# An MLP kernel's start: two weight pieces on ACT's DMA queue, and a shorter row of filling products

## The chip, the cores and the metric

The kernel runs on one core of one Trainium2 chip. The metric is the device time of one execution in microseconds; lower is better. The engines are TensorE (PE, with its weight loads shown as PEld), VectorE (DVE), ScalarE (ACT), GpSimd (POOL) and SyncE (SP), which issues the transfers here. Transfers are carried out by 16 DMA engines that all queues share.

## The reference

A layer norm without parameters, a product with `w1`, a bias, a GELU (tanh form), a product with `w2` and a bias. All tensors are bf16.

```python
B, S, D, F = 1, 2048, 1024, 3584

def reference(x, w1, b1, w2, b2):
    y = _layernorm(x, axis=-1)
    h = _gelu(jnp.einsum("bsd,df->bsf", y, w1) + b1)
    return jnp.einsum("bsf,fd->bsd", h, w2) + b2
```

## The kernel before

The 2048 rows are cut into 16 tiles of 128 rows, and four tiles make a block of 512. For each block the first product makes 28 rows of `hT` (each 128 features by 512 columns, the sum over 8 pieces of D), ACT applies bias and GELU, and the second product makes each tile's output in two halves of 512 columns. DVE adds the second bias and SyncE stores the result. TensorE runs first product, second product, first product and so on, block by block.

The kernel writes a program for each engine by hand: an operation is put at the end of its engine's list with the events that it waits for, and `_emit` (line 74) turns the lists into instructions in that order. Nothing reorders them afterwards, except that DVE's later work is merged by estimated times (line 626 and on).

Only the start matters for this change. It goes like this:

- **Loads.** `LOADS` (line 32) is the order in SyncE's queue behind x tiles 0 and 1. Numbers are pieces of `w1`, negative numbers are x tiles (-2 is tile 2), and `"b1"` is the first bias, which waits for a clearing by GpSimd. The helper `dma` (line 185) records every load, so all have the line L186; it takes a queue `q` and uses SyncE's if there is none. Pieces 0 to 3 hold, for the first, second, third and fourth 128 rows of D, the 1024 columns for the first eight feature rows. Pieces 4 to 7 hold the same rows of D for the next eight feature rows, and pieces 8 to 15 the other four 128-row parts of D. Each of these pieces is 256 KB, as each x tile is. Later pieces are larger.
- **ACT** begins with `preload_act_table` (line 428), which loads the table of the GELU. Behind it stand the sums of tiles 0 and 1 (line 431), each waiting for its x tile; ACT and DVE (line 434) sum a part each.
- **DVE** subtracts the mean from tiles 0 and 1, a part at a time (`centre`, line 439).
- **TensorE** first does filling products on a constant (`fill`, line 295; their result is not used). `fill(n, k)` makes n products of k x 128 columns. Before the change there are nine of 512 columns. Then it turns the first two 128-column parts of tile 0 (`pe_T`, line 300, products with an identity, L311), does two filling products of 128 columns, and follows `OPEN` (line 23). `OPEN` is the list of what TensorE does first: `("T", t, g)` turns a group of parts of tile t, and `(g, t0, t1, d0, d1)` runs the products (L339) of feature group g on tiles t0 to t1 for the parts d0 to d1 of D. So the order is: turn tile 1's first group; eight products of 128 columns with piece 0 on tile 0; turn the second groups of tiles 0 and 1; eight products of 128 columns with piece 0 on tile 1; then 24 products of 256 columns with pieces 1, 2 and 3; then 32 with pieces 4 to 7; then pieces 8 to 11.
- The last four parts of D of tiles 0 and 1 aren't turned by TensorE: DVE turns them in 32 x 32 blocks (line 448), and DVE and ACT move the blocks to their places (`move_half`, line 489, recorded as L494). DVE's twelve of these copies stand behind `mean_tile(2)` (line 478), which waits for x tile 2. The products with pieces 8 to 11 wait for the copies.
- ACT copies each turned group from PSUM to `yT_sb` (L317).

Of the kernel before, what the change touches and what calls it, by code (L numbers as in the profile page):

```python
# [11 lines left out]
P = 128  # L12
# [4 lines left out]
UGROUPS = ((0, 4), (4, 8), (8, 10), (10, 11), (11, 12))  # L17
NPAIR = 2 * UGROUPS[-1][1]
NCEN = 2
N_FILL_A = 9  # L20
N_FILL_C = 2
JT = 4
OPEN = (("T", 1, 0), (0, 0, 1, 0, 1), ("T", 0, 1), ("T", 1, 1), (0, 1, 2, 0, 1), (0, 0, 2, 1, JT), (1, 0, 2, 0, JT),
# [5 lines left out]
          ((0, 2, 6), (2, JT, 4)))  # L29
ACT_BLOCKS_01 = ((0, 1), (0, 2), (1, 2), (1, 3))  # L30
ACT_BLOCKS = ((0, 1), (0, 2), (0, 3), (1, 2), (1, 3), (2, 3))
LOADS = (0, 1, 2, "b1", 3, 4, -2, 5, 6, 7, 8, 9, 10, -3) + tuple(range(11, 22))
NOB = 2
TAIL_CUTS = (0, 384, 512)
N_W2_CHUNKS = 2
# [58 lines left out]
def bass_standalone__mixer_channel_mlp__prompt_kernel(  # L94
# [46 lines left out]
    w1v = w1.rearrange("(t p) f -> p t f", p=P)  # L141
    w2v = w2.rearrange("(t p) d -> p t d", p=P)

    with ExitStack() as es:
        sb = lambda name, shape, dt: es.enter_context(nc.sbuf_tensor(name, shape, dt))

        w1_sb = sb("w1_sb", [P, DT, F], BF16)
# [28 lines left out]
        act = _Prog("s_act")  # L176
# [8 lines left out]
        def dma(dst, src, sig, nbytes, q=None):  # L185
            (q or sp).op(lambda e, dst=dst, src=src: e.dma_start(dst, src), sig=sig, sem="d_" + sig, inc=16)  # L186
            dma_bytes[0] += nbytes
            est[sig] = DMA_T0 + dma_bytes[0] / DMA_BYTES_PER_US

        def load_x_tile(i, q=None):  # L190
            dma(x_sb[:, i, :], xf[i * P:(i + 1) * P, :], f"x{i}", P * D * 2, q)
            x_ev[i] = f"x{i}"
# [4 lines left out]
            for i in range(b0 * TPB, b1 * TPB):  # L197
                x_ev[i] = f"xb{b0}"

        def load_w1(ci):  # L200
            j0, j1, a, b = w1_chunks[ci]
            dma(w1_sb[:, j0:j1, a:b], w1v[:, j0:j1, a:b], f"w1c{ci}", (j1 - j0) * P * (b - a) * 2)

        def load_w2(ci):
            dma(w2_sb[:, ci * W2C:(ci + 1) * W2C, :], w2v[:, ci * W2C:(ci + 1) * W2C, :], f"w2c{ci}",
# [2 lines left out]
        for i in range(2):  # L208
            load_x_tile(i)
        for o in LOADS:  # L210
            if o == "b1":
                sp.op(None, waits=["b1z"])
                dma(b1r_sb[0:FT, :], b1.rearrange("(t p) -> t p", p=P), "b1", F * 2)
            elif o < 0:
                load_x_tile(-o)
            else:
                load_w1(o)
        assert n_open == 1 + max(o for o in LOADS if o != "b1")
        for ci in range(n_open, len(w1_chunks)):
            load_w1(ci)  # L220
# [74 lines left out]
        def fill(n, k):  # L295
            rhs = one.unsqueeze(1).broadcast_to([P, k, P])
            for _ in range(n):
                pe.op(lambda e: e.matmul(ps[:, 0, 0:k * P], lhsT=one, rhs=rhs, start=True, stop=True))  # L298

        def pe_T(i, group, src):  # L300
            blk, t = divmod(i, TPB)
            j0, j1, bank = group
            bap = psb[:, bank, :]
            evs = yT_ev.setdefault(i, [None] * DT)
            for j in range(j0, j1):
                waits = []
                if j == j0:
                    waits = ["ident"] + ([bank_read[bank]] if bank in bank_read else [])
                if j == j0 or y_ev[i][j] != y_ev[i][j - 1]:
                    waits.append(y_ev[i][j])  # L310
                pe.op(lambda e, j=j, o=(j - j0) * P: e.transpose(  # L311
                    out=bap[:, o:o + P], in_=src[:, j * P:(j + 1) * P], identity=ident[:, :]),
                    waits=waits, sig=(f"tp{i}_{j0}" if j == j1 - 1 else None))
                evs[j] = f"te{i}_{j0}"
            psrc = bap[:, 0:(j1 - j0) * P].rearrange("p (j s) -> p j s", j=j1 - j0)
            dst = yT_sb[:, blk % 2, j0:j1, t * P:(t + 1) * P]
            act.op(lambda e, dst=dst, psrc=psrc: e.copy(out=dst, in_=psrc), waits=[f"tp{i}_{j0}"], sig=f"te{i}_{j0}")  # L317
            bank_read[bank] = f"te{i}_{j0}"
            pe_t[0] += (j1 - j0) * 0.056
# [106 lines left out]
            store_last[(ob, region)] = sev  # L426

        act.op(lambda e: e.preload_act_table(ACT.Gelu_apprx_tanh))
        def sums(i, na):
            n2 = (D - na) // 2  # L430
            act.op(lambda e: e.activation(out=hT_sb[:, 2 * NRAW + i, 0:na], in_=x_sb[:, i, 0:na], func=ACT.Copy,
                                          scale=1.0 / D, accum_out=sum_sb[:, 2 * i:2 * i + 1]),
                   waits=[f"x{i}"], sig=f"sa{i}")
            return (lambda e: e.tensor_tensor_reduce(out=o_sb[:, i, 0:n2], in0=x_sb[:, i, na:na + n2],  # L434
                                                     in1=x_sb[:, i, na + n2:D], op0=ALU.add, op1=ALU.add,
                                                     scale=1.0 / D, scalar=0.0, accum_out=sum_sb[:, 2 * i + 1:2 * i + 2]),
                    [f"x{i}"], f"sd{i}")

        def centre(i, j0, j1):
# [4 lines left out]
            y_ev.setdefault(i, []).extend([f"y{i}_{j0}"] * (j1 - j0))  # L444

        sd = [sums(0, SA0), sums(1, HC)]
        def turn_half(i):
            dve_put((lambda e: e.transpose(out=hT_sb[:, NPAIR - 4 + i, :], in_=c_sb[:, i, JT * P:D]), y_ev[i][JT:DT],
# [74 lines left out]
        for q in range(4):  # L523
            f = q ^ 1
# [3 lines left out]
        for h in range(2):  # L528
            f = h ^ 1
# [10 lines left out]
            move(dve, 2, 2, tq, q)  # L540

        fill(N_FILL_A, TPB)
        pe_T(0, GROUPS[0][0], c_sb[:, 0, :])
        fill(N_FILL_C, 1)
        pe_t[0] = T_PE_START
# [81 lines left out]
        ci = fi = 0  # L627
# [57 lines left out]
```

## Time and profile before

| | us |
|---|---|
| median of 3 runs | 396.84 (396.80 to 396.92) |
| the profiled execution, its own time | 396.88 |
| span of that execution, first to last instruction | 395.6 |
| TensorE busy in the span | 392.7 (99%) |
| DVE, ACT busy | 155.6 (39%), 94.4 (24%) |
| granted TensorE clock | 1.00 |
| bytes moved | 23.64 MB, most of them in the first 55 us |

The span is what the profile covers. 1.28 us of the execution's time lie outside of it. The profile has, among other views, the chain of work that ended last, a timeline of each engine, the DMA issues with their time from issue to landing, and the busy time of each engine in a stretch. An instruction group there is named by its line (L339 is line 339 of the kernel), its engine, and the tiles that it writes and reads.

### The profile page before, as it was taken

What the parts mean: (1) busy time and instruction counts of PE and PEld (TensorE: products, weight loads), DVE (VectorE), ACT (ScalarE), POOL (GpSimd) and SP (SyncE); (2) the same over time, 40 slices, a digit from 0 to 9 for tenths busy, and PEclk for the clock granted to TensorE, in tenths of its full rate; (3) what the DMA queues carried; (4) which work ended last, traced back from release to release, by engine and by line L of the source; (5) the groups of instructions that cost most, each with busy time, mean ns of one, the idle gap of its engine ahead of it and who ended that gap; (6) DMA issues with size and microseconds to landing.
All of it is one profiled execution on the core that took longest, in us unless ns stands there. A gap on an engine that the chain in (4) does not pass through costs nothing.

```text
span 395.6 us, 4775 instructions
## 1 busy us (share of the span) xinstructions
PE 392.7 (99%) x2039; PEld 197.6 (50%) x2039; DVE 155.6 (39%) x344; ACT 94.4 (24%) x169; POOL 10.8 (3%) x31
## 2 busy tenths in 40 slices
PE   8999999999999999999999999999999999999998
PEld 5888844444444444444444444444444444444445
DVE  5998989989996005987100000001100000001011
ACT  6787520000144332000023443100003334400000
POOL 1202000110002000000000000000000000000000
DMA  8999940000000000000000000000000000000000
GB/s 284 377 366 384 386 148 22 17 29 13 27 2 0 0 2 0 29 23 17 28 13 0 2 0 0 15 13 27 25 16 15 0 0 2 0 13 28 13 27 28
DMA packets 16190, 23.64 MB, mean 60 GB/s; under 512 B 1194, under 2 KB 8362, under 8 KB 16170
## 3 DMA queue, kind: packets, MB, share of 16 engines
q1 hardware_dynamic: 16170, 23.34, 16.7%
q8 instruction: 16, 0.26, 0.3%
q14 instruction: 4, 0.03, 0.0%
HBM read 19.14 MB, written 4.19 MB: 59 GB/s over the span
## 4 chain that ended last, share of the span: by engine, by line
PE 98%; DMA 1%; SPq 0%; DVE 0%; issue 0%
PE ps L408 49%; PE ps L339 49%; DMA w_sb<-in_w_dram 1%; SPq L186 0%; DVE o_sb L419 0%
## 5 line engine op out<-in xcount | busy, mean ns | idle before, releaser
L339 PE MATMUL ps<-yT_sb,w_sb 128*128 128x512 bf16 (+2 forms) x1096 | 195.0, 340 | 0.1
L408 PE MATMUL ps<-w_sb,hT_sb 128*128 128x512 bf16 (+2 forms) x924 | 194.1, 373 | 0.0
L339 PEld LDWEIGHTS ps<-yT_sb,w_sb 128*128 128x128 bf16 x1096 | 106.3, 98 | 87.8 <-DMA w_sb<-in_w_dram 0.3
L408 PEld LDWEIGHTS ps<-w_sb,hT_sb 128*128 128x128 bf16 x924 | 89.3, 98 | 104.5
L359 ACT ACTIVATE hT_sb<-ps,b_sb 128x512 bf16<-128x512 f32 x88 | 60.5, 688 | 236.3 <-PE ps L339 231.9
L419 DVE TENSOR_TENSOR o_sb<-ps,b_sb 128x512 bf16<-128x512 f32 (+2 forms) x33 | 22.3, 675 | 198.3 <-PE ps L408 198.3
L284 DVE STREAM_TRANSPOSE yT_sb<-x_sb 32x256 bf16<-32x256 bf16 x192 | 83.7, 436 | 28.8 <-PE ps L339 25.8
L380 ACT ACTIVATE hT_sb<-ps,b_sb 128x256 bf16<-128x256 f32 x48 | 18.8, 507 | 8.6 <-PE ps L339 7.3
L237 DVE BATCH_NORM_STATS2 st_sb<-x_sb 128x6 f32<-128x512 bf16 x24 | 15.8, 667 | 0.1
L242 POOL TENSOR_TENSOR rstd_sb<-mv_sb,nhalf 128x1 f32<-128x1 f32 x12 | 6.6, 548 | 100.4 <-DVE mv_sb L245 100.4
L252 DVE TENSOR_SCALAR x_sb<-x_sb,mv_sb,rstd_sb 128x1024 bf16<-128x1024 bf16 x12 | 6.6, 546 | 3.0 <-POOL rstd_sb L242 2.0
L370 DVE TENSOR_TENSOR ps<-ps,rbc_sb 128x512 f32<-128x512 f32 x12 | 7.5, 693 | 0.1
L503 ACT COPY yT_sb<-o_sb 32x256 bf16<-32x256 bf16 x12 | 4.8, 402 | 3.1 <-DVE o_sb L487 2.9
L298 PE MATMUL ps<-const-bfloat16-1.0 128*128 128x512 bf16 (+1 forms) x11 | 4.4, 568 | 0.8 <-PEq L670 0.8
L245 DVE BATCH_NORM_AGGREGATE mv_sb<-st_sb 128x2 f32<-128x15 f32 x12 | 2.7, 223 | 1.2
L503 DVE COPY yT_sb<-o_sb 32x512 bf16<-32x512 bf16 x10 | 2.8, 284 | 0.2
L298 PEld LDWEIGHTS ps<-const-bfloat16-1.0 128*128 128x128 bf16 x11 | 1.4, 139 | 2.7 <-issue 2.7
L494 DVE COPY yT_sb<-hT_sb 32x256 bf16<-32x256 bf16 x12 | 2.6, 218 | 0.1
L487 DVE STREAM_TRANSPOSE o_sb<-c_sb 128x1024 bf16<-128x1024 bf16 x2 | 2.5, 1245 | 0.1
L466 ACT ACTIVATE hT_sb<-x_sb,sum_sb 128x1024 bf16<-128x1024 bf16 x2 | 2.3, 1148 | 0.6 <-DVE sum_sb L478 0.6
L466 ACT ACTIVATE hT_sb<-x_sb,tot_sb 128x1024 bf16<-128x1024 bf16 x2 | 2.3, 1146 | 0.0
L434 DVE CUSTOM_DVE_ANT_0 o_sb<-x_sb 128x384 bf16<-128x384 bf16 (+1 forms) x2 | 1.0, 488 | 3.3 <-DMA x_sb<-in_x_dram 3.3
(33 smaller groups left out, 23.4 us busy)
## 6 DMA issues: line engine op xcount, KB each, us to landing
w_sb<-in_w_dram SPq DMA_DIRECT2D x2, 3584.0 KB, 22.2
w_sb<-in_w_dram SPq DMA_DIRECT2D x18, 256.0 KB, 5.7
out_dram<-o_sb SPq DMA_DIRECT2D x31, 128.0 KB, 1.7
x_sb<-in_x_dram SPq DMA_DIRECT2D x1, 2048.0 KB, 17.1
w_sb<-in_w_dram SPq DMA_DIRECT2D x3, 512.0 KB, 9.9
x_sb<-in_x_dram SPq DMA_DIRECT2D x4, 256.0 KB, 4.0
w_sb<-in_w_dram SPq DMA_DIRECT2D x1, 1024.0 KB, 10.2
x_sb<-in_x_dram SPq DMA_DIRECT2D x1, 1024.0 KB, 11.4
```

The costliest lines, as they stand in the source:

```text
L237: return (lambda e, i=i, h=h: e.bn_stats(st_sb[:, i, 6 * h:6 * (h + 1)], x_sb[:, i, h * HC:(h + 1) * HC]), [x_ev.get(i, f"x{i}_{h}")], f"s ...
L242: pool.op(lambda e, i=i, to=to: e.tensor_tensor(out=to[:, i:i + 1], in0=mv_sb[:, i, 1:2], in1=nhalf[:, i:i + 1], op=ALU.pow), waits=[f"mv{ ...
L252: return (lambda e, i=i: e.tensor_scalar(out=x_sb[:, i, :], in0=x_sb[:, i, :], scalar1=mv_sb[:, i, 0:1], scalar2=rstd_sb[:, i:i + 1], op0= ...
L284: res.append((lambda e, src=src, dst=dst: e.transpose(out=dst, in_=src), waits, (f"tr{i}" if lastop else None), 0.47))
L298: pe.op(lambda e: e.matmul(ps[:, 0, 0:k * P], lhsT=one, rhs=rhs, start=True, stop=True))
L339: pe.op(lambda e, dt=dt: e.matmul(ps[:, bank, o0:o0 + n1 - n0], lhsT=w1_sb[:, dt, r * P:(r + 1) * P], rhs=yT_sb[:, b % 2, dt, n0:n1], star ...
L359: act.op(lambda e, r=r, bank=bank: e.activation(out=hT_sb[:, r, :], in_=ps[:, bank, :], func=ACT.Gelu_apprx_tanh, bias=b1_sb[:, r:r + 1], ...
L370: return (lambda e: e.tensor_tensor(out=pv, in0=pv, in1=rv, op=ALU.mult), [f"mp0_{u}", "rbc"], f"rmp_{u}", 0.70)
L380: act.op(lambda e, r=r, k=k: e.activation(out=hT_sb[:, r, half * NC:(half + 1) * NC], in_=ps[:, bank, k * NC:(k + 1) * NC], func=ACT.Gelu_ ...
L408: pe.op(lambda e, st=st, ft=ft, c0=c0, c1=c1, bank=bank: e.matmul(ps[:, bank, 0:c1 - c0], lhsT=hT_sb[:, ft, st * P:(st + 1) * P], rhs=w2_s ...
L419: crit.append((est[sig], (lambda e, ob=ob, c0=c0, c1=c1, bank=bank: e.tensor_tensor(out=o_sb[:, ob, c0:c1], in0=ps[:, bank, 0:c1 - c0], in ...
L503: op = (lambda e: e.tensor_copy(out=dst, in_=src)) if eng is dve else (lambda e: e.copy(out=dst, in_=src))
```

## The change

Pieces 0 and 2 of `w1` leave SyncE's list. They are issued by ACT, behind its table load and ahead of its first sum. The filling products in front of tile 0 are eight of 512 columns and two of 128, where there were nine of 512. Nothing else differs.

```diff
-N_FILL_A = 9
+N_FILL_A = 8
+N_FILL_B = 2
 N_FILL_C = 2
...
-LOADS = (0, 1, 2, "b1", 3, 4, -2, 5, 6, 7, 8, 9, 10, -3) + tuple(range(11, 22))
+ACT_LOADS = (0, 2)
+LOADS = (1, "b1", 3, 4, -2, 5, 6, 7, 8, 9, 10, -3) + tuple(range(11, 22))
...
-        def load_w1(ci):
+        def load_w1(ci, q=None):
             j0, j1, a, b = w1_chunks[ci]
-            dma(w1_sb[:, j0:j1, a:b], w1v[:, j0:j1, a:b], f"w1c{ci}", (j1 - j0) * P * (b - a) * 2)
+            dma(w1_sb[:, j0:j1, a:b], w1v[:, j0:j1, a:b], f"w1c{ci}", (j1 - j0) * P * (b - a) * 2, q)
...
         act.op(lambda e: e.preload_act_table(ACT.Gelu_apprx_tanh))
+        for ci in ACT_LOADS:
+            load_w1(ci, act)
...
         fill(N_FILL_A, TPB)
+        fill(N_FILL_B, 1)
         pe_T(0, GROUPS[0][0], c_sb[:, 0, :])
         fill(N_FILL_C, 1)
```

## The prediction

> **What bounds the kernel now.** I read the chain of waits first, then the timeline of the first 14 us, then the DMA issues one at a time. The chain shows that TensorE never stops once it has started:
>
> ```profile
> 2.16 4.75 DMA w_sb<-in_w_dram
> 6.91 0.04 issue
> 6.95 48.30 PE ps L339 x408
> ...
> 345.33 48.43 PE ps L408 x252
> 393.76 0.02 issue
> 393.79 0.29 DVE o_sb L419
> ```
>
> (Columns: start, length, what.) From 6.95 us to 393.76 us it is all products of L339 and L408. So this change is worth what it does to the 6.95, as long as nothing behind it starts to wait. What leads up to 6.95 is in the timeline (start, length; idle time before and its releaser in brackets):
>
> ```profile
> 0.78 1.28 ACT L428 ACT_TABLE_LOAD   x1 [0.78 <-PEq L670]
> 0.79 0.85 SPq L186 DMA_DIRECT2D x_sb<-in_x_dram  x2
> ...
> 0.82 4.00 PE L298 MATMUL ps<-const-bfloat16-1.0 128*128 128x512 bf16 x9 [0.82 <-PEq L670]
> ...
> 1.69 1.37 SPq L186 DMA_DIRECT2D w_sb<-in_w_dram  x3
> ...
> 4.17 0.63 ACT L431 ACTIVATE hT_sb<-x_sb 128x512 bf16<-128x512 bf16 x1 [0.36 <-DMA x_sb<-in_x_dram]
> ...
> 4.92 0.80 DVE L440 TENSOR_SCALAR c_sb<-x_sb,sum_sb 128x512 bf16<-128x512 bf16 x2 [0.25 <-ACT hT_sb L431]
> ...
> 5.39 0.11 PEld L311 LDWEIGHTS ps<-ident,c_sb 128*128 128x128 bf16 x2 [0.41 <-DVE c_sb L440]
> ...
> 6.95 9.10 PEld L339 LDWEIGHTS ps<-yT_sb,w_sb 128*128 128x128 bf16 x84 [0.26 <-DMA w_sb<-in_w_dram]
> ```
>
> Two waits end the start-up. The first is on x tile 1: it lands, ACT sums it at 4.17, DVE centres it at 4.92, and TensorE turns it at 5.39. The second, 0.26 us, is on weight piece 1. Had piece 1 been there, the stream would have begun at 6.69.
>
> Landings are issue plus time to landing, asked for each issue alone: x0 0.79 + 2.5 = 3.3; x1 1.22 + 2.9 = 4.1; piece 0 1.69 + 3.6 = 5.3; piece 1 2.16 + 4.7 = 6.9; piece 2 2.63 + 4.9 = 7.5; piece 3 3.62 + 4.6 = 8.2; x2 4.48 + 5.1 = 9.6. From piece 1 on, one 256 KB piece takes about 0.66 us (8.23 less 7.57 in the trace's landing records), while SyncE issues one every 0.47. So issuing is not the limit. The engines that move the bytes are, as the windows show:
>
> ```profile
> 2.00:4.00 2.00, 2.00 (x6) 0.73 (x5) 0.58 (x3) 0.57 (x3) 0.00 (x0) 1.00 1.04 329
> 4.00:4.50 0.50, 0.50 (x2) 0.06 (x1) 0.50 (x2) 0.33 (x1) 0.19 (x1) 1.00 0.85 250
> 4.50:5.00 0.50, 0.50 (x5) 0.41 (x4) 0.25 (x3) 0.39 (x2) 0.03 (x1) 1.00 0.75 279
> ...
> 6.00:8.00 2.00, 1.91 (x26) 1.64 (x24) 1.68 (x4) 1.74 (x5) 0.00 (x0) 1.00 1.04 377
> ```
>
> (The last two columns are the DMA share and GB/s.) The engines are full except for a dip from 4 to 5 us, which makes piece 1 late.
>
> One more limit lies just behind:
>
> ```profile
> 9.63 0.69 DVE L478 CUSTOM_DVE_ANT_0 o_sb<-x_sb 128x512 bf16<-128x512 bf16 x1 [0.74 <-DMA x_sb<-in_x_dram]
> ...
> 10.24 2.76 DVE L494 COPY yT_sb<-hT_sb 32x256 bf16<-32x256 bf16 x12
> ```
>
> The twelve copies behind x2 end at 13.00. TensorE needs them after 24 + 32 products of 256 columns: 56 x 0.109 = 6.10 us after 6.95, at 13.05 (0.109 from the starts 7.07, 7.18, 7.29). It is already held there by 0.03 (starts 12.965 and 13.109). An earlier start than 6.95 is lost again at 13.05 unless x2 also lands earlier.
>
> **The change, part by part.** *The fill.* Nine products of 512 columns, 0.425 us apart (weight loads at 2.06, 2.48, 2.91, 3.34), end at 4.62. Eight end at 4.19, and two of 128 (0.107 apart, starts 4.83 and 4.94) make it 4.40. Tile 0 is centred at 3.99 + 0.34 = 4.33 and its weight load is at 4.45, so its turning can start 0.14 earlier, and so can the copy that now ends at 5.44. But the products behind it stand behind x1's turning at 5.39, which takes to 5.52. Worth at most 0.04 us; I take 0, since x1's wait is the cover. Without that cover it is worth its 0.14. Its price could be the clock: products run at half rate until 4.94 (0.107 for 128 columns) and at full rate from 5.59 (0.055), though the clock column says 1.00 throughout. With less work early, the step may come late (second rival).
>
> *SyncE's queue.* Pieces 0 and 2 leave it. x0 and x1 stay at 0.79 and 1.22, piece 1 moves from 2.16 to 1.69, the bias from 3.11 to 2.16, and everything from piece 3 on goes out some 0.94 earlier (two issues of 0.47). As the bytes ahead of each of them are the same and the engines are full, I take 0 for all from piece 3 on, x2 among them. The dip bounds it: up to 0.3 earlier if the second queue fills it (half a microsecond at 0.85 and half at 0.75 of full is 0.2), 0.3 later if it costs as much again.
>
> *ACT's queue.* Two issues, by SyncE's rows 0.38 to 0.43 each, behind the table load (0.78 to 2.06). ACT's next work, the sum of x0, waits until 3.30, so even 2.06 + 2 x 0.43 = 2.92 delays nothing; that wait is the cover. If an issue cost double there, the sum would come 0.5 late, and so would x0's part.
>
> What decides is when these two go out. GpSimd's first rows start at 0.30, 0.34 and 0.36 with 0.10 each, so an engine's queue passes on the next instruction while one runs. On ACT the trace has a semaphore wait at 7.55 inside the activation from 6.88 to 8.04. So I take it that the DMA issues do not wait for the table load: piece 0 goes out at about 0.83 and piece 2 at about 1.3. By time of issue the order is then x0, piece 0, x1, piece 2, piece 1, where it was x0, x1, 0, 1, 2. On full engines:
> - x1 lands one piece later: 4.14 + 0.66 = 4.80. From its landing to the stream's possible start it took 6.69 - 4.14 = 2.55, so 7.35.
> - Piece 1 is the third weight piece and lands where piece 2 did, at 7.57; with the 0.04 of issue, 7.61.
>
> The later one counts: 7.61 - 6.95 = +0.66. The 0.03 lost at 13.05 comes back, as the copies are then early: **+0.63**. Bounds: 0 if x1 and piece 1 keep their places; +1.07 if both moved pieces pass x1 (4.14 + 1.32 + 2.55 = 8.01).
>
> Later landings have 0.6 us more room with a later start. Span 395.6 + 0.63 = 396.23. This execution took 396.88, 1.28 more than its span, and it stands 0.04 above the median. So 396.23 + 1.28 - 0.04 = 397.47, or 397.5. That is 0.16% slower. A measurement of this kernel can tell about 0.2%, 0.8 us, from no change, so the forecast counts as no change.
>
> **Rivals.**
> *The table load holds the issues.* Piece 0 goes out at 2.07, piece 2 at 2.50, and the move is not an advance. For it: they stand behind it in ACT's program. x1 is then safe. By time of issue piece 1 is ahead of piece 0. Piece 0, one piece later, lands at 5.32 + 0.66 = 5.98 and the stream starts 0.04 + 1.13 later (5.56 to 6.69), at 7.15: +0.2. In the late place that piece 1 has now (6.91) it would be 8.08: +1.1. I take +0.2, 397.0. [...]
>
> *x0 is hit too, and the clock comes late.* If the engines mix both queues evenly, x0 lands at 3.28 + 0.66 = 3.94 and x1 two pieces later, +1.07 in all. TensorE then idles from 4.40 to about 5.1 and again to 6.7. If full speed is missed for that, the 1.13 us of products up to the stream take twice as long: +2.2 at most. I take +1.6, 398.4. It decides when x0's sum starts after 3.9. For it: piece 0 goes out within 0.05 of x0. Against: idle time falls after four busy microseconds. This is the case of slower.
>
> *A gain.* The second queue fills the dip: piece 1 lands by 6.65 and x2 earlier too. At most 0.26 + 0.03: 396.55. Against: both must happen, and x1's path stays.
>
> *A longer hold.* The issues wait on past the load, to about 3.3 (ACT's first row behind it). Piece 0 with its 3.6 lands at 6.9, and the stream starts at 8.07: +1.1, 398.0. [...]
>
> **How the numbers follow.** Forecast 0.45 (own range 396.9 to 397.9), table load holds 0.28, x0 and clock 0.14, gain 0.08, longer hold 0.05. Range 396.6 to 398.2: from the gain to just above the forecast's upper bound (+1.07, less 0.03) and the longer hold; most of the x0 rival lies outside. Slower by over 0.2% starts at 397.63: a fifth of the forecast, most of the x0 rival, the longer hold, a little of the first: 0.30. Faster by over 0.2% would need more than the 0.29 that exists: 0.02. Within 0.2%: 0.68.
>
> **What would show it.** Issues on ACT's queue at 0.8 to 1.7 beside the table load (at 2.07 the first rival); ACT's sum of x1 at about 4.8 instead of 4.17; x0's sum still at 3.30; the first weight load of 256-column products at about 7.6, held by piece 1; the eight products before it at full rate; and from there no wait of TensorE. The forecast is wrong if x1 keeps 4.17, or if x0 moves.

## The result and the profile after

The changed kernel takes 399.25 us (median of 10 runs, 397.65 to 400.40) and the kernel before 396.85 us beside it (10 runs, 396.50 to 397.51). The ratio is 1.0054, with a 95% interval of 1.0038 to 1.0069: slower by 0.5% (this ratio, and those below, are not the quotients of the medians). The single times matter here. They are not spread evenly but stand in three groups: 397.65, 397.69, 397.82; then 399.08, 399.23, 399.27, 399.36; then 400.37, 400.39, 400.40. The profiled execution took 399.36, with a span of 398.1.

The page of the changed kernel has a second queue, and its chain now begins with an x tile:

```profile
q1 hardware_dynamic: 15882, 22.82, 16.2%
q10 hardware_dynamic: 288, 0.52, 0.4%
...
PE 97%; DMA 1%; issue 0%; ACT 0%; DVE 0%; SPq 0%
PE ps L341 49%; PE ps L410 48%; DMA x_sb<-in_x_dram 1%; PE ps L313 0%; ACT hT_sb L435 0%; DVE c_sb L444 0%; SPq L188 0%; DVE o_sb L421 0%
```

(Lines stand two to five further down than before: L341 was L339, L435 was L431.) Queue q10 carries exactly the two moved pieces, 0.52 MB. The timeline of the start (start us, length us; in brackets the idle time before and its releaser):

```profile
0.78 1.28 ACT L430 ACT_TABLE_LOAD   x1 [0.78 <-PEq L675]
0.79 0.86 SPq L188 DMA_DIRECT2D x_sb<-in_x_dram  x2
...
0.81 0.87 ACTq L188 DMA_DIRECT2D w_sb<-in_w_dram  x2
...
4.32 0.42 ACT L435 ACTIVATE hT_sb<-x_sb 128x256 bf16<-128x256 bf16 x1 [2.25 <-DMA x_sb<-in_x_dram]
...
5.48 0.63 ACT L435 ACTIVATE hT_sb<-x_sb 128x512 bf16<-128x512 bf16 x1 [0.66 <-DMA x_sb<-in_x_dram]
...
5.49 0.37 PE L313 MATMUL ps<-ident,c_sb 128*128 128x128 bf16 x2 [0.88 <-DVE c_sb L444]
...
6.71 0.39 PE L313 MATMUL ps<-ident,c_sb 128*128 128x128 bf16 x2 [0.63 <-DVE c_sb L444]
...
6.90 1.06 PE L341 MATMUL ps<-yT_sb,w_sb 128*128 128x128 bf16 x8
```

Two rows of the kernel before, for comparison:

```profile
3.30 0.42 ACT L431 ACTIVATE hT_sb<-x_sb 128x256 bf16<-128x256 bf16 x1 [1.24 <-DMA x_sb<-in_x_dram]
...
5.59 0.61 PE L339 MATMUL ps<-yT_sb,w_sb 128*128 128x128 bf16 x8
```

The DMA issues go out beside the table load, at 0.81. The sum of x0 starts at 4.32, where it was 3.30, and that of x1 at 5.48, where it was 4.17. By the starts of its products TensorE has filling work until 4.40, waits for tile 0 until 5.49, and, after two more filling products, waits from 5.87 for tile 1 until 6.71: 1.9 us in all (the trace's idle times, 0.88 and 0.63, are shorter, since it lets a product last beyond the start of the next). Then comes something that no landing explains: eight products of 128 columns take 1.06 us, where they took 0.61. They start 0.107 apart, against 0.055 before. TensorE is still at half rate, and in the trace it stays there until about 10.2: the trace's clock records, which list the rate that was granted, begin with full rate at 10.23.

The windows of the changed kernel show the DMA engines meanwhile (last two columns: DMA share, GB/s):

```profile
2.00:3.00 1.00, 1.00 (x4) 0.38 (x3) 0.00 (x0) 0.07 (x1) 0.00 (x0) 1.00 0.84 256
3.00:4.00 1.00, 1.00 (x4) 0.36 (x3) 0.00 (x0) 0.00 (x0) 0.00 (x0) 1.00 1.05 404
4.00:5.00 1.00, 0.61 (x3) 0.15 (x1) 0.57 (x2) 0.51 (x2) 0.00 (x0) 1.00 1.05 395
```

In the kernel before they were:

```profile
2.00:3.00 1.00, 1.00 (x4) 0.38 (x3) 0.00 (x0) 0.07 (x1) 0.00 (x0) 1.00 1.09 313
3.00:4.00 1.00, 1.00 (x4) 0.35 (x3) 0.58 (x3) 0.51 (x2) 0.00 (x0) 1.00 1.00 344
4.00:5.00 1.00, 1.00 (x6) 0.47 (x4) 0.75 (x4) 0.72 (x2) 0.23 (x2) 1.00 0.80 264
```

The dip from 4 to 5 us is gone: 395 GB/s there, where the kernel before had 264. The experiments agree: in this stretch the kernels with both pieces on ACT's queue from the start moved 402, 402 and 404 GB/s (the queue alone, more fill, and the changed kernel again), and those with all loads on one queue 223, 272 and 283 (the fill alone, the same order on one queue, and the kernel before with more fill, second time). More bytes are moved from 2 to 5 us (1.06 MB against 0.92), but part of them are weights, which are not what TensorE waits for.

**Where the 2.5 us of span come from.** x1 lands at 5.46 instead of 4.14: +1.32. From tile 1's turning to the first product of 256 columns it takes 2.32 (6.71 to 9.03) instead of 1.56 (5.39 to 6.95): +0.76. That is the sum of 22 small products at half rate (22 x (0.107 - 0.055) = 1.14), less the old wait on piece 1 (0.26) and small gaps. After 9.03 there are still five products of 256 columns at 0.214 and one at 0.18 instead of 0.109: +0.6. Two waits of the kernel before vanish in the later start: 0.03 at 13.0 and 0.22 at 20.1. Together 1.32 + 0.76 + 0.6 - 0.25 = 2.43 of the 2.5.

### The profile page after: what moved, and what is told of

Its sections match the earlier page's. It is cut to its first block, busy times and chain, and to the rows that moved or that the text cites. A ratio compares the mean times of both kernels' runs of the same rounds, so it can differ in the third digit from the quotient of the medians.

```text
span 398.1 us, 4745 instructions
## 1 busy us (share of the span) xinstructions
PE 392.2 (99%) x2008; PEld 199.2 (50%) x2040; DVE 155.4 (39%) x344; ACT 94.4 (24%) x169; POOL 11.1 (3%) x31
## 4 chain that ended last, share of the span: by engine, by line
PE 97%; DMA 1%; issue 0%; ACT 0%; DVE 0%; SPq 0%
PE ps L341 49%; PE ps L410 48%; DMA x_sb<-in_x_dram 1%; PE ps L313 0%; ACT hT_sb L435 0%; DVE c_sb L444 0%; SPq L188 0%; DVE o_sb L421 0%
## 5 line engine op out<-in xcount | busy, mean ns | idle before, releaser
L341 PE MATMUL ps<-yT_sb,w_sb 128*128 128x512 bf16 (+2 forms) x1083 | 195.5, 342 | 0.7
L341 PEld LDWEIGHTS ps<-yT_sb,w_sb 128*128 128x128 bf16 x1096 | 107.8, 99 | 87.3
L313 PE MATMUL ps<-ident,c_sb 128*128 128x128 bf16 x8 | 1.4, 304 | 1.5 <-DVE c_sb L444 1.5
L358 DVE TENSOR_TENSOR ps<-ps,rbc_sb 128x256 f32<-128x256 f32 x4 | 1.7, 432 | 2.9 <-PE ps L341 2.8
```

Source lines behind the costliest of these rows:

```text
L341: pe.op(lambda e, dt=dt: e.matmul(ps[:, bank, o0:o0 + n1 - n0], lhsT=w1_sb[:, dt, r * P:(r + 1) * P], rhs=yT_sb[:, b % 2, dt, n0:n1], star ...
```

## The experiments

Times are medians with the range; the kernel before ran beside each group on the same chip. Its medians were 397.05 (31 runs), 397.27 (35), 397.26 (23) and 397.19 (22) in the four groups.

### Each part alone, more fill, and the same order on one queue

**The fill alone.**

```diff
-N_FILL_A = 9
+N_FILL_A = 8
+N_FILL_B = 2
...
+        fill(N_FILL_B, 1)
```

> The filling products alone are changed (eight of 512 columns and two of 128); all loads stay on SyncE's queue. Theory A (the second queue shares the DMA engines with the x tiles, and TensorE's waits for these tiles then make it miss full speed): nothing is late here, x0's sum starts at 3.30 and x1's at 4.17, products run at full rate from about 5.4, time 396.85 within 0.3. Theory B (the shorter fill by itself is what misses full speed): half-rate products beyond 6 us and 398 or more.

Measured: 397.08 (12 runs, 396.57 to 397.52), ratio 0.9996 (0.9985 to 1.0007). Theory B falls: the shorter fill by itself costs nothing. In the profiled execution products ran at full rate from 5.5 on. Piece 0 happened to land at 6.53 there, and TensorE waited 0.94 for it, still at full rate afterwards (eight products in 0.62).

**The queue alone.** The change without its fill: `ACT_LOADS = (0, 2)` and nine filling products of 512 columns.

> Pieces 0 and 2 go through ACT's queue, the fill stays at nine products of 512 columns. Theory A: x0's sum starts at about 4.3 and x1's at about 5.5 as in the changed kernel, TensorE idles from 4.6 to 5.5 and again to 6.7, and the times spread from 397.7 to 400.4. Theory B: x1 is late in the same way, but full speed comes in time in every run: 397.7.

Measured: 398.41 (12 runs): six from 397.54 to 397.92 and six from 398.90 to 399.60; ratio 1.0033 (1.0018 to 1.0048). The queue part makes the loss, as theory A has it; no run reached the group near 400.4 here (one did when this kernel was run again, further down). The profiled execution (399.60) shows the clock itself. Its windows (the last three columns are the granted clock, the DMA share and GB/s):

```profile
4.00:5.70 1.70, 0.55 (x2) 0.00 (x0) 0.91 (x3) 0.51 (x2) 0.19 (x1) 1.00 1.04 373
5.70:7.40 1.70, 0.84 (x12) 0.69 (x13) 1.32 (x5) 1.11 (x4) 0.19 (x1) 1.00 1.04 378
7.60:10.80 3.20, 3.20 (x24) 2.60 (x22) 3.04 (x11) 2.87 (x8) 0.92 (x2) 0.50 1.05 400
11.00:14.00 3.00, 3.00 (x30) 2.69 (x29) 2.54 (x12) 2.75 (x5) 0.97 (x4) 1.00 1.06 389
```

TensorE had its full clock at 5.7 and lost it again: from 7.6 to 10.8 the granted clock is 0.50, although TensorE is busy the whole time (3.20 of 3.20). In the trace's clock records the half rate lasts 3.41 us, from 7.55 to 10.96, and the full rate before it also 3.41 us, from 4.14. Of the stretch from 4.14 to 7.55 TensorE idled 2.0 us (the TensorE column, of 4.00 to 7.40: 0.55 and 0.84 busy). So the rate was lost 3.41 us after it was granted, 0.6 us after TensorE had begun to work again (6.95). The first grant of full rate does not stand at one time after the start: it is at 4.14 here, at 4.21, 4.29, 4.79 and 4.90 in runs told of below, at 9.54 with one piece on ACT's queue and at 10.23 in the changed kernel above, which fits the groups of times. No trace shows by what the rate is decided. That it is decided at the ends of stretches of 3.41 us, by what TensorE did in them, is an estimate from these lengths, and theory D below is this estimate. The changed kernel's own traces, at the end of this part, show three courses of the clock. How much idling costs the full rate was not measured: with 1.40 us of work from 4.14 to 7.55 it was lost here, and with 1.71 from 4.21 to 7.62 (in the run with one queue below) it was kept.

**The changed kernel with more fill.**

```diff
-N_FILL_A = 8
-N_FILL_B = 2
-N_FILL_C = 2
+N_FILL_A = 10
+N_FILL_B = 3
+N_FILL_C = 14
```

> The changed kernel with more filling products, so that TensorE has work until tile 1 is ready: ten of 512 and three of 128 in front of tile 0 (to about 5.4), fourteen of 128 behind it (to about 6.5 at full rate). Theory A: x0 and x1 are as late as in the changed kernel (sums at 4.3 and 5.5), but products run at full rate from 5.5 on, and all runs lie near 397.7 (+0.8 from the landings alone). If the late landings alone explain the loss, it stays at 399.2.

Measured: 397.78 (12 runs, 397.57 to 397.96), ratio 1.0014 (1.0003 to 1.0026). All twelve lie in the lowest group. Its timeline shows x0 and x1 as late as ever, and the same eight products in 0.61 us:

```profile
4.52 0.42 ACT L435 ACTIVATE hT_sb<-x_sb 128x256 bf16<-128x256 bf16 x1 [2.46 <-DMA x_sb<-in_x_dram]
...
5.69 0.63 ACT L435 ACTIVATE hT_sb<-x_sb 128x512 bf16<-128x512 bf16 x1 [0.66 <-DMA x_sb<-in_x_dram]
...
7.04 0.61 PE L341 MATMUL ps<-yT_sb,w_sb 128*128 128x128 bf16 x8
```

This splits the loss. The landings alone cost 397.78 - 397.05 = 0.73 us. The rest of the changed kernel's loss is half rate: filling products that compute nothing take it away, and the clock records have full rate from 4.90 on.

**The same order of issue on one queue.**

```diff
         for i in range(2):
             load_x_tile(i)
+            load_w1(2 * i)
...
-LOADS = (0, 1, 2, "b1", 3, 4, -2,
+LOADS = (1, "b1", 3, 4, -2,
```

> All loads on SyncE's queue, in the order of issue that the changed kernel has: x0, piece 0, x1, piece 2, piece 1, bias, piece 3 and so on; the fill is that of before. Theory A: without a second queue x0 is back at 3.3 and x1 one piece late at about 4.8 (sum at 4.85), the stream starts at about 7.6, and the time is 397.3 to 397.6 if full speed comes in time. Theory C (the order of bytes does it, not the two queues): x0 at 4.3 and x1 at 5.5, 397.7 to 400.4.

Measured: 399.62 (8 runs): 397.63, 398.30, five from 399.50 to 400.95, and 401.19; ratio 1.0056 (1.0033 to 1.0078). Both theories are half right. In the timeline of its lowest run x0 is back, but x1 is not at 4.8:

```profile
3.60 0.42 ACT L432 ACTIVATE hT_sb<-x_sb 128x256 bf16<-128x256 bf16 x1 [1.54 <-DMA x_sb<-in_x_dram]
...
5.45 0.63 ACT L432 ACTIVATE hT_sb<-x_sb 128x512 bf16<-128x512 bf16 x1 [1.34 <-DMA x_sb<-in_x_dram]
...
6.68 0.28 PE L312 MATMUL ps<-ident,c_sb 128*128 128x128 bf16 x2 [1.50 <-DVE c_sb L441]
```

The transfer in third place lands late even on one queue: here it is x1, at 5.43, and in the kernel before it was piece 0, at 5.32, 1.2 after x1 (4.14). So one piece ahead of x1 is worth 1.2 to 1.3 and not 0.66. This lowest run kept full rate from 4.21 on. Seven of the eight runs are slower, which a wait of 1.5 us that costs the full rate in most runs would explain: four of the seven have a mean granted clock of 0.996, where this run has 1.00, but none of them left a trace. Without two queues the order of bytes makes a loss of the same size.

### Which gap matters, the kernel before with more fill, and one piece

**Only the gap in front of tile 0 filled:** `N_FILL_A = 10`, `N_FILL_B = 3`, `N_FILL_C = 2`.

> The changed kernel with filling products up to tile 0 only (ten of 512 and three of 128 columns, to about 5.4); the gap in front of tile 1, from 5.9 to 6.7, stays. Theory D (full speed is granted or taken at the edges of stretches of 3.41 us, by how busy TensorE was in the whole stretch, and the edges fall anywhere): with only 0.8 us idle no stretch is idle enough, nearly all runs at 397.5 to 398.0. Theory E (any gap of 0.8 us is enough to miss it): the spread of the changed kernel, 397.7 to 400.4.

Measured: 397.81 (11 runs): ten from 397.55 to 398.00, one at 399.54. The forecast of theory D held.

**Only the gap in front of tile 1 filled:** `N_FILL_A = 8`, `N_FILL_B = 2`, `N_FILL_C = 10`.

> The changed kernel with ten instead of two filling products behind tile 0 (to about 6.7 at half rate); the gap in front of tile 0, from 4.4 to 5.5, stays. Theory D: the loss is part repaired, since 1.1 us idle remain of the 1.9: median between 397.8 and 398.8, with some runs at 399. Theory E: the spread of the changed kernel.

Measured: 398.78 (11 runs): five from 397.63 to 397.79, six from 398.78 to 399.54. Five of 11 lie in the lowest group, against 8 of 27 of the changed kernel in its three series, so a repair is not clear here. Against the 10 of 11 of the run before, it points to the earlier and longer gap as the one that counts most, but these counts don't settle it.

**The kernel before with six filling products behind tile 0, twice:** `N_FILL_C = 6`.

> The kernel before with six instead of two filling products behind tile 0, so that TensorE has work up to tile 1 at 5.39. If the scatter of the kernel before comes from full speed arriving late, its runs draw together near 396.5 to 396.8. If it comes from late weight pieces alone, nothing changes: 396.85 with the same scatter. Half-rate filling products could hold tile 1 up by 0.1.

> The kernel before with six filling products behind tile 0, a second time beside more runs of the kernel before. If the larger times of the kernel before (near 399) are runs in which full speed is missed, this kernel has fewer of them: at most 1 run of 12 above 398.5. If its 12 runs without one were luck, about a quarter lies near 399.

Measured: 397.18 (12 runs, 396.81 to 397.55), ratio 0.9986 (0.9970 to 1.0001), and the second time 397.19 (11 runs, 396.50 to 397.99), ratio 0.9998 (0.9985 to 1.0010). The median doesn't move by what can be measured. But the kernel before had runs above 398.5 on these chips, 9 of 35 and 2 of 23, and this one had none of 23. So it may avoid a late clock, if that is what those runs of the kernel before had (none of them left a trace); with these counts that is likely but not settled, and no faster kernel is shown. The runs didn't draw together near 396.6 either; pieces that land late would explain it.

**Piece 2 alone on ACT's queue:** `ACT_LOADS = (2,)`, piece 0 back behind x1.

> The changed kernel with piece 2 alone on ACT's queue; piece 0 goes back to SyncE's queue behind x1. One piece of 256 KB now shares the DMA engines with x0 and x1 where there were two. Theory A: x0 still shares from its middle on, 0.5 to 0.9 late (sum at 3.9 to 4.2); x1 0.6 to 0.8 late (sum at 4.8 to 5.0); 397.3 to 398.5, between before and the changed kernel. If it is the moved piece 0 that costs the time, it is 396.9.

Measured: 399.20 (11 runs, 397.71 to 399.40), ratio 1.0028 (1.0010 to 1.0046). One piece does as much harm as two, which theory A did not expect. The sums in its profiled execution:

```profile
4.75 0.42 ACT L435 ACTIVATE hT_sb<-x_sb 128x256 bf16<-128x256 bf16 x1 [2.68 <-DMA x_sb<-in_x_dram]
...
5.55 0.63 ACT L435 ACTIVATE hT_sb<-x_sb 128x512 bf16<-128x512 bf16 x1 [0.29 <-DMA x_sb<-in_x_dram]
```

x0 is later than with two pieces, and from 2 to 4 us the engines moved 205 and 301 GB/s. Why they were slower there stays open. Full rate came at 9.54. It is clear that the move of piece 0, which is back in its place, is not needed for the loss.

### ACT issuing later

**Pieces 0 and 2 behind ACT's sum of x0.**

```diff
         act.op(lambda e: e.preload_act_table(ACT.Gelu_apprx_tanh))
-        for ci in ACT_LOADS:
-            load_w1(ci, act)
...
-        sd = [sums(0, SA0), sums(1, HC)]
+        sd = [sums(0, SA0)]
+        for ci in ACT_LOADS:
+            load_w1(ci, act)
+        sd.append(sums(1, HC))
```

> The changed kernel, but ACT issues pieces 0 and 2 behind its sum of x0 (at about 3.4) instead of behind the table load. If the loss comes from the second queue running beside the x tiles, x0's sum is back at 3.3 to 3.6 and x1's at 4.2; piece 0 is then the late one: issued at 3.4 it lands at 5.9 to 6.6 and the stream starts at 7.1 to 7.8, so 397.0 to 397.8 with few runs at 399. If the second queue costs time wherever it stands, 399 as in the changed kernel.

Measured: 402.36 (4 runs, 401.87 to 403.14), ratio 1.0133 (1.0112 to 1.0153). The x tiles are back (sums at 3.28 and 4.32), but piece 0 lands far later than either theory had it:

```profile
3.29 0.39 ACTq L188 DMA_DIRECT2D w_sb<-in_w_dram  x1
...
9.02 1.04 PE L341 MATMUL ps<-yT_sb,w_sb 128*128 128x128 bf16 x8 [3.19 <-DMA w_sb<-in_w_dram]
```

It takes 5.7 us from issue to landing, behind what SyncE had already issued (the piece that SyncE issued at 3.05 also took 5.7 and landed at 8.76, this one at 8.98). TensorE waits 3.2 for it, and goes on at half rate (granted clock 0.50 from 7.62 to 14.45).

**A try at a better kernel: piece 1 alone behind the sum of x0.** As above with `ACT_LOADS = (1,)`, piece 0 first in SyncE's list, nine filling products of 512 columns and six of 128 behind tile 0.

> A try at a better kernel: only piece 1 goes through ACT's queue, issued behind the sum of x0 (at about 3.4), so that the two queues run together from 4 to 5 us, where one queue moved 250 to 280 GB/s; fill of nine products of 512 columns, six of 128 behind tile 0. If the second queue fills that dip and leaves x0 and x1 alone, piece 1 lands by 6.6 and x2 earlier, and the median is 0.1 to 0.3 below that of the kernel with more fill alone. If piece 1 shares with pieces 0 and 2, it lands at 6.8 or later and nothing is gained.

Measured: 398.62 (12 runs, 397.92 to 401.00), ratio 1.0045 (1.0027 to 1.0063). It failed: piece 1, issued at 3.47, took 5.3 us, and the first product of 256 columns waited for it until 8.79.

```profile
8.79 5.41 PE L341 MATMUL ps<-yT_sb,w_sb 128*128 128x256 bf16 x48 [1.69 <-DMA w_sb<-in_w_dram]
```

### The changed kernel again, and beside the queue alone

> The changed kernel on the chip of this call, so that it stands beside the others and the kernel before. Groups near 397.7, 399.2 and 400.4 again, median near 399.2; if the groups belong to the phase of the clock's stretches, their shares may differ from the first time.

Measured: 399.11 (5 runs): 397.81, then 398.88 to 399.45. The groups are there; none of these runs was near 400.4. The profiled run was the one of 397.81, and it parts the clock from the landings in one and the same kernel. x1 landed at 5.61, later than the 5.46 of the run of 399.36, and the waits were as long; but full rate was granted at 4.79 instead of 10.23, and the eight products took 0.61:

```profile
5.63 0.63 ACT L435 ACTIVATE hT_sb<-x_sb 128x512 bf16<-128x512 bf16 x1 [0.67 <-DMA x_sb<-in_x_dram]
...
6.98 0.61 PE L341 MATMUL ps<-yT_sb,w_sb 128*128 128x128 bf16 x8
```

The last two stand side by side on one chip, since the prediction had given the fill a price in the clock.

> The changed kernel beside the kernel with the queue part alone, on one chip. If the shorter fill (0.21 us less in front of tile 0) makes full speed come late more often, this one's median lies 0.5 us or more above the other's and it has fewer runs near 397.7. If it is nothing, as the prediction had it, the two share one spread.

> Pieces 0 and 2 on ACT's queue with nine filling products of 512 columns. If the shorter fill matters, about half of the runs lie near 397.7 here and at most a third in the changed kernel; if not, the shares are alike.

Measured: 399.05 with the shorter fill (12 runs, four below 398) and 399.15 without (12 runs, five below 398, one at 400.62). They share one spread. The fill has no measurable part in the loss, with or without the second queue; the difference seen between the two in separate series before may have been chance. The profiled run of the changed kernel here, of 399.92, has the third course of the clock: full rate from 4.29, and lost from 7.70 to 11.11 after 1.0 us of work in the 3.41 us before (granted clock in the third column from the end):

```profile
7.80:11.00 3.20, 3.20 (x25) 2.71 (x23) 3.04 (x11) 2.67 (x7) 0.63 (x1) 0.50 1.05 388
```

No run near 400.4 left a trace, so what the clock did in that group is not shown.

## Why the prediction was wrong

- **What bounds the kernel** was right: the time follows the start of TensorE's stream, and nothing behind it waits in the changed kernel.
- **The issues beside the table load** were right: 0.81 and 1.23 against 0.83 and about 1.3. The rivals in which the table load holds them fell.
- **"x1 lands one piece later: 4.14 + 0.66 = 4.80"** was mis-sized. It landed at 5.46, 1.32 later. The 0.66 is the spacing of pieces 2 and 3 (7.57 and 8.23), with the engines full (DMA share 1.04 from 6 to 8). The place that x1 was moved into was that of the third transfer, and the row for it stood in the same list: piece 0 landed 1.2 after x1. The one-queue run shows that this place is enough for x1's delay, without a second queue (5.43 there).
- **That x0 keeps 3.30** was wrong: 4.32. In the trace the transfers of 2 KB of the two queues run mixed (270 on q1 and 245 on q10 between 2 and 5 us), and x0 and piece 0, started together, end almost together, at 4.30 and 4.48. The second rival had this, and x1's delay of two pieces (1.32) too. x0 landed 1.02 later than alone (4.30 against 3.28). The trace doesn't name the engine of a transfer, so how a single engine takes turns between the queues is not shown.
- **"Piece 1 lands where piece 2 did, at 7.57"** was wrong in the other direction: 6.45, with the dip filled. Part of this may be scatter: with the same order of loads on one queue piece 0 landed at 5.32 in the kernel before and at 6.53 in the run with the fill alone. An early piece 1 was the gain of the third rival, but x1's path was longer by then. Nor is the wait of 0.26 on piece 1, on which the forecast stood, there in every execution: in the second run of the kernel before with more fill TensorE was busy all of 5 to 7 us (1.00 in both windows, against 0.86 and 0.91).
- **The landings together** were forecast at +0.63 and are worth +0.73 (the run with more fill, all at one rate; its span is 1.0 above that of the one execution that the prediction started from). That the sum is near is partly luck. The path that counted was not piece 1's (7.61) but x1's: 5.46 + 2.55 = 8.01, which is +1.06 and not the 7.35 of the prediction. What brings it down again are 0.03 and 0.22 of later waits that vanish; the prediction had counted the first alone.
- **The clock at no cost** is the step that failed. The prediction let full speed come in time with a chance of about 0.85, and named x1's wait as the cover for the fill. But that wait is idle time, and idle time is what costs the full rate here: of the +2.40, 0.73 are landings and about 1.7 are half rate. The second rival had the mechanism, with +1.6 taken and +2.2 as the most; the median is +2.4 and the highest group +3.5. It was given 0.14 and stood mostly outside the range. Against it I had put that the idling falls after four busy microseconds. That is no protection, in two ways: in the run of 399.36 full rate was not granted before 10.23, and in the run with the queue alone it was had at 4.14 and lost again 3.41 us later.
- **The shorter fill at 0** was right (397.08 alone, and no difference beside the queue).

## What to carry to other kernels

In a start-up, count what each late transfer leaves TensorE idle, not only what it delays: here landings worth 0.7 us cost 2.4, because 1.9 us of idling kept the full rate from coming or took it away again for 3.41 us. The second DMA queue raised the bytes moved here (395 GB/s against 264 from 4 to 5 us), but it took them from what was urgent on the first (x0 1.02 us later), so only what is needed no sooner than the first queue's head should start beside it. When one kernel's times stand in groups, read the start of products in the profile before averaging: a run with enough filling products tells landing time from clock time.

## What was not expected of the hardware

- Full rate can be lost after it was granted: in the run with the queue alone it held for 3.41 us and fell to 0.50 for another 3.41 us while TensorE was working, as it did in a run of the changed kernel (4.29, 7.70 and 11.11).
- The clock column did not show the half rate at the beginning: it says 1.00 from 3 to 5 us in the changed kernel, while products were 0.107 apart for 128 columns. The trace's clock records begin with the first grant, and the column takes all time before as 1.00. Only the later fall shows as 0.50. The distance of products tells it in both cases.
- A piece of 256 KB issued on ACT's queue at 3.3 to 3.5, behind what SyncE had issued until then, took 5.7 and 5.3 us to land, while pieces that SyncE issued at 3.6 and 4.0 in the kernel before took 4.6 and 4.9. It is not that ACT's queue is the slower one: in the same two runs SyncE's pieces issued at 3.05 and 3.53 took 5.7 and 5.4.
- The kernel before itself had runs above 398.5 on some chips (9 of 35 in one group, none of the first 10). In its kept trace the start leaves TensorE idle for only 0.4 us before tile 1.
